# Weight conversion on VectorE and ScalarE alone, in 768-column jobs, in a gated linear attention with a feed-forward layer

## The chip, the cores and the metric

The kernel runs on one core of a Trainium2 chip. The metric is the device time of one execution in microseconds, as a median over executions; lower is better. A difference under about 0.5% (3 us here) can't be told from no change.

## The reference

The first stage is a gated linear attention over 4 batches, 8 heads, 768 time steps and head size 48. The second is a feed-forward layer over the 3072 tokens with 384 features each and an inner width of 2048. The two weights come in double precision, 8 bytes a number; everything else is float32.

```
for t in range(S):
    state = alpha[:, :, t, :, None] * state + einsum('bhd,bhe->bhde', k[:, :, t], v[:, :, t])
    y[:, :, t] = einsum('bhd,bhde->bhe', q[:, :, t], state)
x = y.transpose(0, 2, 1, 3).reshape(B * S, H * D)
h = x @ w_in
g = maximum(0.01 * h, h)
out = g @ w_out
```

## The kernel before

**Attention.** Time is cut into 6 chunks of 128 steps; a unit is one chunk of one batch, 24 in all, and three units make a block of 384 tokens. For a unit the generator `attention` yields eight slices of work: `scans` (running products of alpha on VectorE, L255 and L260), `scores` (TensorE, L292), `mask_scores` (one half masked by GpSimd at L299, one by VectorE at L302), `k_tokens` (L310), `scaled_q` and `scaled_k`, `outputs` (L326 and L332 on TensorE, then the float32r parts `xh` on ScalarE and `xl` on VectorE, L339), and `next_state` (the products of keys and values on TensorE, L353, then the state update by VectorE, L362, and GpSimd, L363). The first six units turn their inputs by TensorE (L227), the others by VectorE (L231). When the third unit of a block has its `xl`, `gather` sends six DMAs (L372) that complete the block's input, and the block is ready for the feed-forward.

**Feed-forward.** Every float32 number is split into a high and a low float32r part, and a product is three matmuls. An item (i, f) is slice f (128 of the 2048 inner columns, 16 slices) of block i (8 blocks): `ffn_in` does nine matmuls into `ph` (L413), ScalarE and VectorE make `t`, `gh`, `gl` (L416 to L421), and `ffn_out` does nine matmuls (L429), two items later (`LAG`).

**Weights.** Each of the 16 slices needs its part of `w_in` and of `w_out`. They are loaded as pairs of 32-bit words and turned into a high and a low part by integer work: 32 jobs of 384 columns, odd and even for the two weights, in three stages with a load ahead of them. Per job ScalarE does three operations (L177, L179, L200), VectorE three (L197, L198, L199), GpSimd two (L201, L202), and the last addition (L209) falls to GpSimd for odd jobs and to VectorE for even ones. Three buffers (`NRAW`) of 384 columns hold loaded words.

**Order of the work.** The program lists items in this order, with jobs and slices of attention between them, and a scheduler then sets each engine's order:

```
items = [(0, f, 2, SL / (CATCH - 1)) for f in range(CATCH)]
for n in range(LEAD):
    items += [(0, CATCH + n, 1, 0), (1, n, 1, 0)]
items += [(1, LEAD + n, 0, SL / (CATCH - 1) if n else 0) for n in range(CATCH)]
items += [(i, f, 0, SL / NF) for i in range(2, NB) for f in range(NF)]
```

The third entry is the number of calls of `convert`, the fourth the slices of attention beside the item. With `CATCH` 9 the first block runs alone for nine slices, then blocks 0 and 1 take turns for seven, then block 1 runs its last nine. Attention stops after unit 5 and goes on when block 0 is finished; the first five slices of it are held behind `gl` of item (0, 14) (`held`, `tc.issue_after`).

Of the kernel before, what the change touches and what calls it, by code (L numbers as in the profile page):

```python
# [22 lines left out]
def gated_linear_attn_ffn(ctx, tc, q, k, v, alpha, w_in, w_out, out):  # L23
# [30 lines left out]
    NREST, NBITS, NPW = 3, 3, 2  # L54
    NRAW = 3
# [4 lines left out]
    CATCH = 9  # L60
# [26 lines left out]
    wih, wil, woh, wol, x_sb = pieces("large", F32R, (NG, DF), (NG, DF), (NF, DM), (NF, DM), (2, 2 * NG + 1, TB))  # L87
# [65 lines left out]
    def load_weights(j):  # L153
        f, second = divmod(j, 2)
        wd = I64 if f64 else F32
        raw = cvp.tile([P, NG, 2 * P], I32, name="raw", bufs=NRAW)
        if second:
            dst = raw.rearrange("p g f -> p (g f)").bitcast(wd) if f64 else raw[:, :, 0:P].bitcast(F32)
            src = w_out[f * P:(f + 1) * P, :]
            nc.sync.dma_start(dst, src if f64 else src.rearrange("p (g f) -> p g f", g=NG))  # L160
        else:
            dst = raw.bitcast(wd) if f64 else raw[:, :, 0:P].bitcast(F32)
            for r, n, src, step in runs:
                a = w_in[src:src + n, f * P:(f + 1) * P]
                nc.sync.dma_start(
                    dst[r:r + n], bass.AP(a.tensor, a.offset, [list(a.ap[0]), [step * DF, NG], list(a.ap[1])])
                )
        jobs[j] = [raw]

    def convert_1(j):  # L170
        if not f64:
            return
        raw, = jobs[j]
        words = raw.rearrange("p g (f w) -> p g f w", w=2)
        top, low = words[:, :, :, 1], words[:, :, :, 0]
# [4 lines left out]
        jobs[j] = top, rest  # L180

    def convert_2(j):
        f, second = divmod(j, 2)
        if second:
            hi, lo = (w[:, f, :].rearrange("p (g f) -> p g f", g=NG) for w in (woh, wol))
        else:
            hi, lo = (w[:, :, f * P:(f + 1) * P] for w in (wih, wil))
        if not f64:
            val = jobs.pop(j)[0][:, :, 0:P].bitcast(F32)
            nc.scalar.copy(hi, val)  # L190
            nc.gpsimd.tensor_tensor(lo, val, hi.bitcast(F32), ALU.subtract)
            return
        top, rest = jobs[j]
        bits = cvp.tile([P, NG, P], I32, name="bits", bufs=NBITS)
        val = bits.bitcast(F32)
        pw = cvp.tile([P, NG, P], I32, name="pw", bufs=NPW)
# [3 lines left out]
        nc.scalar.copy(hi, val)  # L200
        nc.gpsimd.tensor_tensor(rest, pw.bitcast(F32), rest, ALU.mult)  # L201
        nc.gpsimd.tensor_tensor(val, val, hi.bitcast(F32), ALU.subtract)  # L202
        jobs[j] = lo, rest, val

    def convert_3(j):
        if f64:
            lo, rest, val = jobs.pop(j)
            eng = nc.gpsimd if j % 2 else nc.vector
            eng.tensor_tensor(lo, rest, val, ALU.add)  # L209

    NJ = 2 * NF

    def convert(h):
        for ahead, stage in ((5, convert_1), (4, convert_2), (2, convert_3), (8, load_weights)):
            if 0 <= h + ahead < NJ:
                stage(h + ahead)
# [98 lines left out]
    def outputs(u):  # L315
# [20 lines left out]
        del masked[u]  # L336
        xh, xl = (x_sb[0:BR, n, at:at + NP, j * C:(j + 1) * C] for n in (0, 1))
# [3 lines left out]
    def next_state(u):  # L341
        tb, b = units[u]
        pe, _, ktok = live.pop(u)[:3]
        V, W = vals_sb[u % NV], state[b]
        if tb == NC - 1:
            load_values(u + NV)
            return
        kv = bank()[:, 0:NP * D].rearrange("d (p e) -> d p e", p=NP)
        us = atp.tile([P, NP, D], F32, name="us") if tb else None
        for s, lo in ((0, 0), (1, HB)):  # L350
            for p in range(NP):
                h = 2 * p + s
                nc.tensor.matmul(  # L353
                    kv[lo:lo + D, p, :], ktok[:, p, lo:lo + D], V[:, h * D:(h + 1) * D], start=True, stop=True
                )
        load_values(u + NV)
# [49 lines left out]
    def ffn_in(i, f):  # L406
        xh, xl = xs[i]
        ph = ps_h.tile([P, 512], F32, name="ph")[:, 0:TB]
        fs = slice(f * P, (f + 1) * P)
        n = 0  # L410
        for g in range(NG):
            for wt, xt in ((wih, xh), (wih, xl), (wil, xh)):
                nc.tensor.matmul(ph, wt[:, g, fs], xt[:, g, :], start=n == 0, stop=n == 3 * NG - 1)  # L413
                n += 1
# [9 lines left out]
    def ffn_out(po, gs, f):  # L424
        gh, gl = gs
        for j in range(UPB):
            js = slice(j * C, (j + 1) * C)
            for n, (gt, wt) in enumerate(((gh, woh), (gh, wol), (gl, woh))):
                nc.tensor.matmul(  # L429
                    po[j], gt[:, js], wt[:, f, :], start=f == 0 and n == 0, stop=f == NF - 1 and n == 2  # L430
# [11 lines left out]
    for n in range(12):  # L442
        next(st)
        if n >= 4:
            convert(n - 12)
# [177 lines left out]
```

## Time and profile before

| | |
|---|---|
| median of 3 runs | 596.2 us (594.42 to 597.63) |
| the profiled execution | 594.61 us, of which the span is 592.9 us |
| busy share | PE 93%, weight loads 87%, DVE 70%, ACT 42%, POOL 23% |
| mean granted TensorE clock | 0.965 of 2.4 GHz |

The profiled execution is 1.6 us (0.3%) under the median. Busy shares are means over stages that differ: the first 220 us hold the weight conversion and nine units of attention, the rest is blocks 2 to 7 with the other units. A row of a timeline gives the start, the length, the engine, the line, the tiles, the number of merged instructions, and in brackets the idle time before it and what ended it. Rows of consecutive VectorE operations overlap by a little: the distance between two starts is what an operation holds the engine for.

### The profile page before, as it was taken

What the parts mean: (1) busy time and instruction counts of PE and PEld (TensorE: products, weight loads), DVE (VectorE), ACT (ScalarE), POOL (GpSimd) and SP (SyncE); (2) the same over time, 40 slices, a digit from 0 to 9 for tenths busy, and PEclk for the clock granted to TensorE, in tenths of its full rate; (3) what the DMA queues carried; (4) which work ended last, traced back from release to release, by engine and by line L of the source; (5) the groups of instructions that cost most, each with busy time, mean ns of one, the idle gap of its engine ahead of it and who ended that gap; (6) DMA issues with size and microseconds to landing.
All of it is one profiled execution on the core that took longest, in us unless ns stands there. A gap on an engine that the chain in (4) does not pass through costs nothing.

```text
span 592.9 us, 10070 instructions
## 1 busy us (share of the span) xinstructions
PE 550.6 (93%) x3706; PEld 516.1 (87%) x3706; DVE 414.2 (70%) x759; ACT 249.5 (42%) x541; POOL 138.7 (23%) x178
## 2 busy tenths in 40 slices
PE   5865989699999999999999999999999999999995
PEld 3754979598898879999999999999999989999995
DVE  6899999998999999356847775757757543333331
ACT  3666656554454335333534344333433243334332
POOL 3587679876001121011101001001101000000000
PEclk9877798889999999999999999999999999999998
DMA  9996763510434565014412251222311220011001
GB/s 164 209 192 165 168 170 89 158 50 1 112 109 103 127 137 135 22 39 83 116 37 62 60 131 45 62 51 59 102 26 39 46 67 0 2 21 40 2 1 44
DMA packets 90087, 48.11 MB, mean 81 GB/s; under 512 B 49584, under 2 KB 87984, under 8 KB 90032
## 3 DMA queue, kind: packets, MB, share of 16 engines
q1 hardware_dynamic: 90032, 47.41, 35.2%
q8 instruction: 31, 0.51, 0.3%
q14 instruction: 24, 0.20, 0.1%
HBM read 40.30 MB, written 4.72 MB: 76 GB/s over the span
## 4 chain that ended last, share of the span: by engine, by line
PE 64%; DVE 18%; DMA 7%; SPq 3%; issue 3%; POOL 1%; ACT 1%; DVEq 0%; ACTq 0%; POOLq 0%
PE ph L413 27%; PE a L429 27%; PE b L292 3%; PE b L332 2%; PE b L326 2%; DVE gl L421 2%; DVE bits L197 2%; DMA raw<-in_moe_w_in_dram 2%; DVE large L209 2%; DVE bits L198 2%; DMA large<-large 1%; DMA raw<-in_moe_w_out_dram 1%; DVE pc L255 1%; DMA small<-in_v_dram 1%; PE b L353 1%
## 5 line engine op out<-in xcount | busy, mean ns | idle before, releaser
L413 PE MATMUL ph<-large 128*128 128x384 f32 x1152 | 232.9, 346 | 9.6 <-DVE t L417 6.7
L413 PEld LDWEIGHTS ph<-large 128*128 128x128 f32 x1152 | 206.3, 193 | 15.8 <-DVE t L417 8.7
L429 PE MATMUL a<-large,gh 128*128 128x384 f32 x672 | 174.4, 344 | 0.0
L417 DVE TENSOR_TENSOR t<-ph,t 128x384 f32<-128x384 f32 x128 | 70.4, 552 | 100.3 <-ACT t L416 99.6
L429 PEld LDWEIGHTS a<-large,gh 128*128 128x128 f32 x672 | 119.3, 188 | 4.2 <-ACT gh L419 0.7
L416 ACT ACTIVATE t<-ph 128x384 f32<-128x384 f32 x128 | 62.4, 490 | 139.1 <-PE ph L413 131.2
L429 PE MATMUL a<-large,gl 128*128 128x384 f32 x336 | 110.7, 339 | 0.0
L421 DVE TENSOR_TENSOR gl<-t,gh 128x384 fp32r<-128x384 f32 x128 | 80.8, 632 | 39.6 <-ACT gh L419 37.5
L419 ACT CAST gh<-t 128x384 fp32r<-128x384 f32 x128 | 65.3, 513 | 80.2 <-DVE t L417 80.1
L363 POOL TENSOR_TENSOR small<-us,pe 48x192 f32<-48x192 f32 x32 | 18.3, 572 | 192.5 <-DVE us L362 191.8
L429 PEld LDWEIGHTS a<-large,gl 128*128 128x128 f32 x336 | 62.8, 188 | 0.2
L201 POOL TENSOR_TENSOR rest<-pw,rest 128x384 f32<-128x384 f32 x32 | 36.8, 1148 | 30.8 <-DVE pw L199 29.3
L299 POOL TENSOR_SCALAR_AFFINE_SELECT sm<-sm 128x512 f32<-128x512 f32 x24 | 17.5, 731 | 90.1 <-ACT sm L298 90.1
L202 POOL TENSOR_TENSOR bits<-bits,large 128x384 f32<-128x384 f32 x32 | 38.3, 1197 | 0.0
L266 ACT ACTIVATE e<-pc 128x512 f32<-128x512 f32 x24 | 15.2, 632 | 38.2 <-DVE rc L260 30.0
L292 PEld LDWEIGHTS b<-qs,ks 48*128 48x128 f32 x288 | 22.5, 187 | 8.7 <-issue 6.8
L292 PE MATMUL b<-qs,ks 48*128 48x128 f32 x288 | 28.4, 289 | 1.7 <-DVE us L362 0.8
L255 DVE TENSOR_TENSOR_SCAN pc<-e,small 128x128 f32<-128x128 f32 x72 | 25.5, 414 | 0.4
L429 PE MATMUL b<-large,gh 128*128 128x384 f32 x96 | 23.3, 345 | 2.1 <-ACT gh L419 2.1
L200 ACT CAST large<-bits 128x384 fp32r<-128x384 f32 x32 | 16.3, 511 | 20.5 <-DVE bits L198 20.2
L198 DVE SCALAR_TENSOR_TENSOR bits<-raw,bits 128x384 int32<-128x384 int32 x32 | 24.8, 789 | 0.2
L227 PE MATMUL a<-small 128*128 128x128 f32 x72 | 15.6, 367 | 8.9 <-POOL small L142 3.3
(80 smaller groups left out, 613.2 us busy)
## 6 DMA issues: line engine op xcount, KB each, us to landing
raw<-in_moe_w_out_dram SPq DMA_DIRECT2D x16, 384.0 KB, 3.8
small<-in_v_dram SPq DMA_DIRECT2D x24, 192.0 KB, 3.0
raw<-in_moe_w_in_dram SPq DMA_DIRECT2D x32, 144.0 KB, 3.9
out_dram<-t SPq DMA_DIRECT2D x24, 192.0 KB, 2.2
small<-in_alpha_dram SPq DMA_DIRECT2D x38, 96.0 KB, 2.3
small<-in_k_dram SPq DMA_DIRECT2D x36, 96.0 KB, 2.2
small<-in_q_dram SPq DMA_DIRECT2D x36, 96.0 KB, 2.2
small<-in_alpha_dram SPq DMA_DIRECT2D x36, 80.0 KB, 2.4
```

What stands on the lines that cost most here:

```text
L198: nc.vector.scalar_tensor_tensor(bits, top, -0x80000000, bits, ALU.bitwise_and, ALU.bitwise_or)
L201: nc.gpsimd.tensor_tensor(rest, pw.bitcast(F32), rest, ALU.mult)
L202: nc.gpsimd.tensor_tensor(val, val, hi.bitcast(F32), ALU.subtract)
L255: nc.vector.tensor_tensor_scan(pc[:, p, :], aT[:, p, :], ones.broadcast_to([P, C]), 1.0, ALU.mult, ALU.mult)
L292: nc.tensor.matmul(ss[s][:, p, :], ks[lo:lo + D, p, :], qs[lo:lo + D, p, :], start=True, stop=True)
L363: nc.gpsimd.tensor_tensor(W[r, :, r], us[r], pe[r].broadcast_to([D, NP, D]), ALU.mult)
L413: nc.tensor.matmul(ph, wt[:, g, fs], xt[:, g, :], start=n == 0, stop=n == 3 * NG - 1)
L416: nc.scalar.mul(t, ph, 0.01)
L417: nc.vector.tensor_tensor(t, ph, t, ALU.max)
L419: nc.scalar.copy(gh, t)
L421: made[i, f] = nc.vector.tensor_tensor(gl, t, gh.bitcast(F32), ALU.subtract)
L429: nc.tensor.matmul(po[j], gt[:, js], wt[:, f, :], start=f == 0 and n == 0, stop=f == NF - 1 and n == 2)
```

## The change

All of the conversion's GpSimd work goes to VectorE, and one job now holds slice f of both weights side by side, 768 columns wide: for one slice of both weights ScalarE does two operations of 768 columns instead of six of 384, and VectorE six of 768 columns instead of seven of 384. The low words are scaled and multiplied in one VectorE operation. The load buffers stay three, each twice as wide; the weights lie in `wh` and `wl` with both parts of a slice beside each other. `CATCH` goes from 9 to 6, with one `convert` call for each of the first 26 items, of which the first 15 still find a stage to run. In `outputs` the eight products of keys and values (`kv`) are issued right behind the value products, ahead of `xh` and `xl`, and in pairs of halves; before they were issued in the slice after.

```diff
-    CATCH = 9
+    CATCH = 6
...
-    def load_weights(j):
-        f, second = divmod(j, 2)
+    def load_weights(f):
...
-        raw = cvp.tile([P, NG, 2 * P], I32, name="raw", bufs=NRAW)
+        raw = cvp.tile([P, 2 * NG, 2 * P], I32, name="raw", bufs=NRAW)
...
-        rest = cvp.tile([P, NG, P], F32, name="rest", bufs=NREST)
-        nc.scalar.activation(rest, low.bitcast(U32), AF.Copy, scale=2.0 ** -52)
         nc.scalar.mul(top.bitcast(F32), top.bitcast(F32), 2.0 ** -112)
...
+        bits = cvp.tile([P, 2 * DM], I32, name="bits", bufs=NBITS)
+        pw = cvp.tile([P, 2 * DM], I32, name="pw", bufs=NPW)
         nc.vector.tensor_scalar(bits, top, 3, 0x7FFFFFF8, ALU.logical_shift_left, ALU.bitwise_and)
         nc.vector.scalar_tensor_tensor(bits, top, -0x80000000, bits, ALU.bitwise_and, ALU.bitwise_or)
+        nc.scalar.copy(hi, val)
         nc.vector.tensor_scalar(pw, bits, -0x800000, None, ALU.bitwise_and)
-        nc.scalar.copy(hi, val)
-        nc.gpsimd.tensor_tensor(rest, pw.bitcast(F32), rest, ALU.mult)
-        nc.gpsimd.tensor_tensor(val, val, hi.bitcast(F32), ALU.subtract)
+        nc.vector.scalar_tensor_tensor(rest, low.bitcast(U32), 2.0 ** -52, rest, ALU.mult, ALU.mult)
...
-            eng = nc.gpsimd if j % 2 else nc.vector
-            eng.tensor_tensor(lo, rest, val, ALU.add)
+            nc.vector.tensor_tensor(val, val, hi.bitcast(F32), ALU.subtract)
+            nc.vector.tensor_tensor(lo, rest, val, ALU.add)
...
     def convert(h):
-        for ahead, stage in ((5, convert_1), (4, convert_2), (2, convert_3), (8, load_weights)):
+        for ahead, stage in ((2, convert_1), (2, convert_2), (1, convert_3), (4, load_weights)):
...
+                    nc.tensor.matmul(
+                        kv[lo:lo + D, p, :], ktok[:, p, lo:lo + D], V[:, h * D:(h + 1) * D], start=True, stop=True
+                    )
+        load_values(u + NV)
+        live[u] = pe, kv
         xh, xl = (x_sb[0:BR, n, at:at + NP, j * C:(j + 1) * C] for n in (0, 1))
         nc.scalar.copy(xh, y[0:BR])
...
-        if n >= 4:
-            convert(n - 12)
+        if n in (4, 6, 8, 10):
+            convert(n // 2 - 6)
...
-    items = [(0, f, 2, SL / (CATCH - 1)) for f in range(CATCH)]
+    items = [(0, f, 1, SL / (CATCH - 1)) for f in range(CATCH)]
```

Three places show what the scheduler makes of it. In the kernel before, VectorE's last conversions lie among the feed-forward's operations (`t` and `gl` of an item), and three pairs follow the last one (L209) until the attention of unit 6 begins (L231):

```order
L199 TENSOR_SCALAR pw_1580<-bits_1579 128x384
L417 TENSOR_TENSOR t_1525<-ph_1515,t_1525 128x384
L421 TENSOR_TENSOR gl_1530<-t_1525,gh_1528 128x384
L209 TENSOR_TENSOR large_74<-rest_1503,bits_1544 128x3x128
L417 TENSOR_TENSOR t_1563<-ph_1553,t_1563 128x384
L421 TENSOR_TENSOR gl_1568<-t_1563,gh_1566 128x384
```

In the changed kernel VectorE's order behind the `xl` of unit 5 (L347, the operation that lets block 1's input be gathered) holds only conversions for a while: the slices of jobs 10 to 13 stand there and no item of the feed-forward:

```order
L347 TENSOR_TENSOR large_74<-a_797,large_74 112x4x128
L208 TENSOR_TENSOR large_74<-pw_1006,bits_1005 128x768
L201 SCALAR_TENSOR_TENSOR pw_1048<-raw_972,pw_1048 128x768
L207 TENSOR_TENSOR bits_1047<-bits_1047,large_74 128x768
L197 TENSOR_SCALAR bits_1089<-raw_1014 128x768
L208 TENSOR_TENSOR large_74<-pw_1048,bits_1047 128x768
L198 SCALAR_TENSOR_TENSOR bits_1089<-raw_1014,bits_1089 128x768
L197 TENSOR_SCALAR bits_1131<-raw_1056 128x768
L200 TENSOR_SCALAR pw_1090<-bits_1089 128x768
L198 SCALAR_TENSOR_TENSOR bits_1131<-raw_1056,bits_1131 128x768
L201 SCALAR_TENSOR_TENSOR pw_1090<-raw_1014,pw_1090 128x768
```

Seven items of the feed-forward have their `gl` ahead of this place; in the kernel before eight had it ahead of the same `xl`. Further on in the changed kernel, behind the last conversion, nine pairs of `t` and `gl` stand alone before the attention of unit 6 begins (L228); the last two are these:

```order
L415 TENSOR_TENSOR t_1438<-ph_1428,t_1438 128x384
L419 TENSOR_TENSOR gl_1443<-t_1438,gh_1441 128x384
L415 TENSOR_TENSOR t_1464<-ph_1454,t_1464 128x384
L419 TENSOR_TENSOR gl_1469<-t_1464,gh_1467 128x384
L228 STREAM_TRANSPOSE e_1610<-small_73 128x4x4x32
L228 STREAM_TRANSPOSE qs_1630<-small_73 128x4x4x32
```

So the conversions moved forward and the `gl` of item (0, 14), which is the last before L228 in either kernel, became the 23rd item's instead of the 20th's. On TensorE the third place is unit 7 in the kernel before, where the products of keys and values (L353) stand behind nine matmuls of the feed-forward:

```order
L326 MATMUL b<-qs,small 112x128 x4
L332 MATMUL b<-sm,small 48x128 x8
L413 MATMUL ph<-large 128x384 x9
L353 MATMUL b<-small,ktok 48x48 x8
L429 MATMUL a<-large,gh 128x384 x2
```

In the changed kernel they follow the value products of the same unit:

```order
L323 MATMUL b<-qs,small 112x128 x4
L329 MATMUL b<-sm,small 48x128 x8
L340 MATMUL b<-small,ktok 48x48 x8
L411 MATMUL ph<-large 128x384 x9
```

From block 2 to the end TensorE goes back and forth between feed-forward and attention 104 times in the changed kernel and 120 times in the one before.

## Rows read from the trace of the kernel before

**Rows 1.** The page, part 1: busy time of each engine, share of the span, instructions.

```profile
PE 550.6 (93%) x3706; PEld 516.1 (87%) x3706; DVE 414.2 (70%) x759; ACT 249.5 (42%) x541; POOL 138.7 (23%) x178
```

**Rows 2.** Busy time of each engine by stretch, granted clock, DMA share, GB/s.

```profile
61.00:105.00 44.00, 40.32 (x272) 38.26 (x270) 42.62 (x70) 26.40 (x58) 34.01 (x32) 0.90 0.56 137
105.00:151.00 46.00, 39.82 (x196) 37.72 (x197) 40.91 (x60) 22.93 (x49) 33.00 (x29) 0.89 0.25 67
151.00:209.40 58.40, 54.91 (x407) 51.15 (x405) 57.31 (x113) 25.39 (x60) 6.38 (x15) 1.00 0.49 120
...
278.00:343.50 65.50, 65.50 (x469) 61.63 (x468) 44.30 (x84) 25.89 (x57) 6.07 (x12) 1.00 0.32 75
```

**Rows 3.** Groups of VectorE instructions from 15 to 151 us: count | busy, mean ns.

```profile
L198 DVE SCALAR_TENSOR_TENSOR bits<-raw,bits 128x384 int32<-128x384 int32 x32 | 24.8, 789 | 0.2
L421 DVE TENSOR_TENSOR gl<-t,gh 128x384 fp32r<-128x384 f32 x20 | 19.6, 978 | 4.5 <-ACT gh L419 4.5
L197 DVE TENSOR_SCALAR bits<-raw 128x384 int32<-128x384 int32 x32 | 18.4, 588 | 0.8 <-ACT raw L179 0.8
L209 DVE TENSOR_TENSOR large<-rest,bits 128x384 fp32r<-128x384 f32 x16 | 17.8, 1116 | 0.1
L199 DVE TENSOR_SCALAR pw<-bits 128x384 int32<-128x384 int32 x32 | 16.7, 534 | 0.1
```

**Rows 4.** Groups of VectorE instructions from 240 us to the end.

```profile
L421 DVE TENSOR_TENSOR gl<-t,gh 128x384 fp32r<-128x384 f32 x90 | 50.6, 564 | 34.1 <-ACT gh L419 31.9 <-PE a L429 2.0
```

**Rows 5.** Timeline of VectorE: operations that start back to back.

```profile
29.21 0.55 DVE L198 SCALAR_TENSOR_TENSOR bits<-raw,bits 128x384 int32<-128x384 int32 x1
29.68 0.35 DVE L197 TENSOR_SCALAR bits<-raw 128x384 int32<-128x384 int32 x1
29.95 0.72 DVE L360 TENSOR_TENSOR small<-a,pe 48x192 f32<-48x192 f32 x2
...
52.44 0.68 DVE L275 TENSOR_TENSOR qs<-a,pc 128x512 f32<-128x512 f32 x1
53.04 0.68 DVE L283 TENSOR_TENSOR ks<-a,rc 128x512 f32<-128x512 f32 x1
```

**Rows 6.** Timeline of VectorE: an even job's last addition, and one held up.

```profile
78.70 0.54 DVE L209 TENSOR_TENSOR large<-rest,bits 128x384 fp32r<-128x384 f32 x1
...
102.16 1.36 DVE L209 TENSOR_TENSOR large<-rest,bits 128x384 fp32r<-128x384 f32 x1
```

**Rows 7.** Timeline of VectorE: marks of units 5 and 8, item (0, 14), block 2.

```profile
104.20 0.69 DVE L339 TENSOR_TENSOR large<-a,large 112x512 fp32r<-112x512 f32 x1
...
150.25 0.56 DVE L421 TENSOR_TENSOR gl<-t,gh 128x384 fp32r<-128x384 f32 x1 [0.58 <-ACT gh L419]
...
208.73 0.69 DVE L339 TENSOR_TENSOR large<-b,large 112x512 fp32r<-112x512 f32 x1
...
219.94 0.55 DVE L417 TENSOR_TENSOR t<-ph,t 128x384 f32<-128x384 f32 x1
```

**Rows 8.** Timeline of TensorE: after an idle stretch, and a change to attention and back.

```profile
118.23 6.13 PE L413 MATMUL ph<-large 128*128 128x384 f32 x18 [2.79 <-DVE t L417]
...
386.46 1.16 PE L292 MATMUL b<-qs,ks 48*128 48x128 f32 x16
387.55 0.62 PE L429 MATMUL a<-large,gh 128*128 128x384 f32 x2
...
388.18 0.51 PE L429 MATMUL a<-large,gh 128*128 128x384 f32 x2
```

**Rows 9.** DMA issues of SyncE for a gather; landing times of all gathers, 40 to 130 us.

```profile
45.40 3.07 SPq L372 DMA_DIRECT2D large<-large  x4
...
DMA to landing us min/median/max: 2.1/2.2/3.3
```

**Rows 10.** The chain that ended last, near the end: start, length, what.

```profile
559.49 1.59 PE a L429 x9
561.08 1.56 PE ph L413 x9
```

More of the change, by code (lines that the diff above doesn't have):

```diff
@@ L53, in gated_linear_attn_ffn @@
     NV = 2
-    NREST, NBITS, NPW = 3, 3, 2
-    NRAW = 3
+    NBITS, NPW, NRAW = 2, 2, 3
     T4 = 4
@@ L170, in convert_1 @@
-    def convert_1(j):
+        raw = cvp.tile([P, 2 * NG, 2 * P], I32, name="raw", bufs=NRAW)
+        if f64:
+            dst = raw.bitcast(wd)
+        else:
+            dst = raw[:, :, 0:P].bitcast(wd)
+        for r, n, src, step in runs:
+            a = w_in[src:src + n, f * P:(f + 1) * P]
+            nc.sync.dma_start(
+                dst[r:r + n, 0:NG], bass.AP(a.tensor, a.offset, [list(a.ap[0]), [step * DF, NG], list(a.ap[1])])
+            )
+        nc.sync.dma_start(dst[:, NG:], w_out[f * P:(f + 1) * P, :].rearrange("p (g f) -> p g f", g=NG))
@@ L171, in convert_1 @@
+        jobs[f] = [raw]
+    def convert_1(f):
         if not f64:
             return
-        raw, = jobs[j]
-        words = raw.rearrange("p g (f w) -> p g f w", w=2)
-        top, low = words[:, :, :, 1], words[:, :, :, 0]
-        rest = cvp.tile([P, NG, P], F32, name="rest", bufs=NREST)
-        nc.scalar.activation(rest, low.bitcast(U32), AF.Copy, scale=2.0 ** -52)
-        nc.scalar.mul(top.bitcast(F32), top.bitcast(F32), 2.0 ** -112)
[L180 to L187, printed above, removed]
-        if not f64:
-            val = jobs.pop(j)[0][:, :, 0:P].bitcast(F32)
-            nc.scalar.copy(hi, val)
-            nc.gpsimd.tensor_tensor(lo, val, hi.bitcast(F32), ALU.subtract)
+        raw, = jobs[f]
+        words = raw.rearrange("p g (f w) -> p (g f) w", w=2)
+        top, low = words[:, :, 1], words[:, :, 0]
+        nc.scalar.mul(top.bitcast(F32), top.bitcast(F32), 2.0 ** -112)
+        jobs[f] = top, low
@@ L342, in next_state @@
         tb, b = units[u]
[L343 to L346, printed above, removed]
+        pe, kv = live.pop(u)
+        if kv is None:
             return
-        kv = bank()[:, 0:NP * D].rearrange("d (p e) -> d p e", p=NP)
+        W = state[b]
         us = atp.tile([P, NP, D], F32, name="us") if tb else None
[L350 to L356, printed above, removed]
         for lo in (0, HB):
@@ L408, in ffn_in @@
         ph = ps_h.tile([P, 512], F32, name="ph")[:, 0:TB]
-        fs = slice(f * P, (f + 1) * P)
         n = 0
         for g in range(NG):
-            for wt, xt in ((wih, xh), (wih, xl), (wil, xh)):
-                nc.tensor.matmul(ph, wt[:, g, fs], xt[:, g, :], start=n == 0, stop=n == 3 * NG - 1)
+            for wt, xt in ((wh, xh), (wh, xl), (wl, xh)):
+                nc.tensor.matmul(ph, w_in_of(wt, f, g), xt[:, g, :], start=n == 0, stop=n == 3 * NG - 1)
                 n += 1
@@ L427, in ffn_out @@
             js = slice(j * C, (j + 1) * C)
-            for n, (gt, wt) in enumerate(((gh, woh), (gh, wol), (gl, woh))):
+            for n, (gt, wt) in enumerate(((gh, wh), (gh, wl), (gl, wh))):
                 nc.tensor.matmul(
-                    po[j], gt[:, js], wt[:, f, :], start=f == 0 and n == 0, stop=f == NF - 1 and n == 2
+                    po[j], gt[:, js], w_out_of(wt, f), start=f == 0 and n == 0, stop=f == NF - 1 and n == 2
                 )
@@ L584, in stepwise @@
                     nc.vector.tensor_tensor(gl, g, gh.bitcast(F32), ALU.subtract)
-                    for n, (gt, wt) in enumerate(((gh, woh), (gh, wol), (gl, woh))):
-                        nc.tensor.matmul(po, gt, wt[:, f, :], start=f == 0 and n == 0, stop=f == NF - 1 and n == 2)
+                    for n, (gt, wt) in enumerate(((gh, wh), (gh, wl), (gl, wh))):
+                        nc.tensor.matmul(po, gt, w_out_of(wt, f), start=f == 0 and n == 0, stop=f == NF - 1 and n == 2)
                 o = gp.tile([P, DM], F32, name="o")
```

52 lines of the change are left out of this document (27 added, 25 removed).

## The prediction

> **What bounds the kernel now.** I read the busy times by stretch first, then the groups of VectorE, then the two timelines around the places where the attention of one block must be complete before the next block can begin. From block 2 on the kernel is a TensorE kernel: a block with three units beside it takes 65.5 us, TensorE is busy in all of them at the full clock, and VectorE has 21 us to spare [rows 2]. An item costs 1.56 us for its first nine matmuls and 1.59 for the other nine [rows 10]. Nothing that VectorE gains there moves the end. The first 220 us are different. From 61 to 209.4 us VectorE is busy 140.8 of 148.4 us, TensorE 135.1, the latter in part at a granted clock of 0.9 [rows 2]. So the front is VectorE's, with TensorE close behind, and what counts is when three marks are reached [rows 7]: the `xl` of unit 5 (104.2 us), which lets block 1 begin; the `gl` of item (0, 14), over at 150.8 us, behind which the attention of units 6 to 8 is held; and the `xl` of unit 8 (208.7 us), after which block 2's first `t` comes at 219.9. I price the change at each mark.
>
> **What the conversion costs VectorE.** GpSimd's 138.7 us [rows 1] are mostly conversion, and they are not free for VectorE: the same addition of 384 columns takes 0.54 us at one place and 1.36 at another [rows 6], and `gl` takes 978 ns on average while the conversion runs and 564 after it [rows 3, 4]. In the stretch of the conversion VectorE spends 24.8 + 18.4 + 16.7 + 17.8 = 77.7 us on it [rows 3]. Undisturbed, an operation with two inputs holds the engine for 0.47 us at 384 columns (29.21 to 29.68) and 0.60 at 512 (52.44 to 53.04), so 1.04 ns a column and 0.87 us at 768; the one with a constant 0.27 at 384 (29.68 to 29.95), so 0.47 at 768 at the same 0.07 of fixed time [rows 5]. A new job is two of the second kind and four of the first: 0.94 + 3.48 = 4.4 us, 16 jobs 70.7 us. The old ones overlap their neighbours by some 0.08 us each (0.55 against 0.47), 112 of them 9 us, so they held the engine for about 69. The conversion itself therefore costs VectorE the same as before; taking the work over is paid for by the blocking that goes away. The gain is on `gl`: 20 times 0.41, 8.3 us. The operation that scales the low words has no row; its bounds are 0.47 us (the cheap kind) and 1.36 (the held-up kind at 384), and I take 0.87 since it reads two tensors as L198 does: 16 times the difference is -6 to +8 us.
>
> The Trainium skill, in "SBUF — State Buffer", section "Who interferes with whom", says why: GpSimd and VectorE's second port are one pair, and an operation with two SBUF inputs that meets a GpSimd operation reading SBUF is blocked for the whole of it. By that rule the selects and state updates that stay on GpSimd could each still block one of the long new operations, at 0.7 us each some 8 us over the eleven units in the front. The row speaks for less: from 240 us on the same selects and updates run beside 90 `gl` that take 564 ns on average, next to the shortest seen [rows 4, 5]. The sum goes by the row, at nothing.
>
> **First mark.** Up to the `xl` of unit 5 the old order has 22 jobs' three stages and 11 additions on VectorE, the new one 12 jobs' first three operations, 11 of the next two each and 10 of the last. Old: 22 times (0.789 + 0.588 + 0.534 - 3 times 0.08) plus 11 times 1.03, 48 us [rows 3]. New: 12 times (0.94 + 0.87) plus 32 times 0.87, 49.6 us. Items: eight pairs of `t` and `gl` at 0.47 + 0.90, 11 us, against seven at 0.94, 6.6. That is 2.8 us less, 101.4. New waits come in: the second job needs all of both weights of slice 1 at about 20 us, when only half of that was needed before, and the transposes of unit 4 stand on TensorE behind the first 18 matmuls of the feed-forward. I put 1.5 and 1 us on them and come to 104 us; bounds 101 (no wait) and 107 (each twice as long, and one of TensorE's clock restarts in it).
>
> **Second mark.** This is where `CATCH` costs. The 23rd item's `gl` is now the one that releases attention, not the 20th's, and 16 items' first matmuls stand between block 1's gather and it. From the `xl`: two DMA issues at 0.77 us and 2.2 to land [rows 9], 3.7 us. Then TensorE has 16 times 1.56 and 13 times 1.59 to do, 45.6 us [rows 10]. It stood idle for some 5 us before, since VectorE then does conversions only (the second fence on the order); before, after 2.8 us idle, 18 matmuls took 6.13 us where two times 1.56 is 3.1 [rows 8], so 3 us more. Then `t` to `gl`, four operations of about 0.55 us, 2.2. Sum 54.5 us, and the mark lies at 158.5 us instead of 150.8: +7.7. VectorE's own work in that stretch (26 us of conversions and seven pairs, and then nine pairs that wait for TensorE at 3.15 us an item) ends within a microsecond or two of the same time, so neither is far off the path.
>
> **Third mark.** Between the two marks VectorE was busy 57.3 of 58.4 us [rows 2]. Its work there is the same but for three pairs of `t` and `gl` that are now done earlier (2.8 us) and a transpose and a few small operations that stand later (1.3 us): -4.1. From the `xl` of unit 8 to block 2's first `t` the new order has about 1.2 us less on VectorE: -1.2. Behind that everything is TensorE's. It changes 16 times less between attention and feed-forward; a change and back costs 0.1 us at 386.46 (the items before end at 386.36) and 0.11 on return (0.62 against 0.51) [rows 8], so 8 pairs save 1.7 us. And some 15 small products of unit 9 are already done, 0.7 us. This is what the move of the `kv` products is worth; the pairing of halves I price at nothing, since each keeps its weight load.
>
> **Sum.** +7.7 - 4.1 - 1.2 - 1.7 - 0.7 = 0.0 us on a profile of 594.6 us. The median of before lies 1.6 us higher, at 596.2, and so does the forecast: 596.2 us. VectorE loses its obstruction, and the time comes back as TensorE's: conversions that run ahead of need, then fourteen items in a row that nothing can shorten.
>
> **Rivals.** *Faster, 0.30:* the front is not stopped by TensorE. If the first mark comes at 101 and TensorE isn't cold when block 1 begins (its 3 us), the second mark falls at 152.5 and the end at 590. The 8.3 us of `gl` and GpSimd's freedom speak for it (masks and state updates no longer queue behind 1.2 us operations); TensorE's 40.3 busy of 44 us from 61 to 105 speaks against it [rows 2]. *Slower, 0.27:* VectorE is stopped by what TensorE owes it. It takes its list in order, and with GpSimd gone every conversion now stands in that one list: a `t` whose `ph` is late holds back the slice that a later `ph` needs. The place is from the first items to the end of the conversions, where VectorE had 1.4 us idle of 44 [rows 2]. If it waits 3 us more ahead of the first mark and 3 more behind it, the end is at 602; from 1.5 us in each it is measurable. *No difference, 0.43:* the sum. Loads bring the same bytes; by the sum the conversions end near 131 us where the last one now ends near 145, so they are wanted at a rate about a tenth higher than now, and a slice that comes late counts with the slower case.
>
> **Range.** The low end takes the faster rival and a cheaper scale operation, 588.5; the high end the slower one and some of the remaining blocking, 604. Faster by over 0.5% 0.30, same 0.43, slower 0.27; 3 us is about the least that can be told here.
>
> **What would show it.** The new operations at 0.95 us (0.87 held) and `gl` at 0.56 from the start; GpSimd's busy time near 35 us; the `xl` of unit 5 at 101 to 107; TensorE at a low clock just after, and then without a gap while VectorE idles for nine items; the `gl` before the transposes at 156 to 161; unit 8's `xl` at 210 to 214; blocks of about 65 us. It is wrong if the long operations are held up by what is left on GpSimd, if VectorE shows waits for `ph` or raw data of over 6 us from 20 to 130 us, or if attention starts well ahead of 155.

## The result and the profile after

The changed kernel takes 600.88 us (median of 6 runs, 598.73 to 602.2) against 596.58 us before (6 runs): ratio 1.0076, 95% interval 1.0049 to 1.0103. It is slower by 4.3 us, where no change was forecast; the time lies inside the range. The profiled execution of after took 602.2 us (span 600.4), that of before 594.6: 7.6 us between the two, and these are what the marks below add up to. The first lies 1.3 us above its median and the second 2.0 below, so 3.3 of the 7.6 us are spread between executions and not the change. All times are medians; in one experiment a single execution of 1685 us is left out.

The page of after, busy time of each engine (answers to [rows 1]):

```profile
PE 552.5 (92%) x3706; PEld 521.5 (87%) x3706; DVE 406.2 (68%) x743; ACT 231.2 (39%) x477; POOL 51.6 (9%) x98
```

GpSimd has lost 87 us and VectorE is not busier. Busy time by stretch for after (answers to [rows 2]: PE, PEld, DVE, ACT, POOL, granted clock, DMA share, GB/s):

```profile
0.00:61.00 61.00, 36.17 (x229) 29.50 (x230) 50.79 (x98) 24.09 (x43) 10.84 (x26) 0.72 1.00 176
61.00:105.00 44.00, 39.56 (x298) 36.93 (x297) 43.02 (x74) 21.51 (x39) 5.35 (x8) 0.92 0.67 151
105.00:165.00 60.00, 52.86 (x277) 52.58 (x278) 39.39 (x63) 21.38 (x39) 0.71 (x1) 0.89 0.19 48
165.00:220.00 55.00, 51.23 (x375) 46.20 (x373) 52.44 (x105) 22.83 (x54) 6.52 (x14) 0.98 0.52 124
...
137.00:165.00 28.00, 28.00 (x161) 28.00 (x160) 10.32 (x19) 9.05 (x18) 0.00 (x0) 1.00 0.00 1
```

The third row and the last are the new thing: for 60 us VectorE is busy 39.4, and in the last 28 of them TensorE runs without a gap while VectorE is busy for 10.3. Before, VectorE had 40.9 busy of 46 us there [rows 2].

VectorE's groups of after from 15 to 165 us (answers to [rows 3]):

```profile
L198 DVE SCALAR_TENSOR_TENSOR bits<-raw,bits 128x768 int32<-128x768 int32 x16 | 15.5, 967 | 0.0
L208 DVE TENSOR_TENSOR large<-pw,bits 128x768 fp32r<-128x768 f32 x16 | 15.4, 962 | 0.1
L201 DVE SCALAR_TENSOR_TENSOR pw<-raw,pw 128x768 f32<-128x768 uint32 x16 | 15.2, 950 | 0.0
L207 DVE TENSOR_TENSOR bits<-bits,large 128x768 f32<-128x768 f32 x16 | 15.2, 949 | 0.3 <-ACT large L199 0.3
L415 DVE TENSOR_TENSOR t<-ph,t 128x384 f32<-128x384 f32 x23 | 12.7, 552 | 15.4 <-ACT t L414 15.4
L419 DVE TENSOR_TENSOR gl<-t,gh 128x384 fp32r<-128x384 f32 x23 | 12.7, 554 | 5.8 <-ACT gh L417 5.7
L197 DVE TENSOR_SCALAR bits<-raw 128x768 int32<-128x768 int32 x16 | 9.2, 577 | 2.8 <-ACT raw L181 2.7 <-DMA large<-large 0.2
L200 DVE TENSOR_SCALAR pw<-bits 128x768 int32<-128x768 int32 x16 | 8.8, 550 | 0.1
```

The six groups of the conversion (L197 to L208) add up to 79.3 us, against 77.7 before; less 0.08 us of overlap for each of the 96 operations it is 71.6 us held, and 70.7 were forecast. `gl` fell from 978 to 554 ns. So every operation has the price that it was given. What moved is when things are reached. The marks of after in VectorE's timeline, `xl` of units 1, 2, 3 and 5, the last `gl` ahead of the held attention, `xl` of unit 8, and block 2's first `t` (answers to [rows 7]):

```profile
37.72 0.68 DVE L347 TENSOR_TENSOR large<-a,large 112x512 fp32r<-112x512 f32 x1
55.55 0.69 DVE L347 TENSOR_TENSOR large<-a,large 112x512 fp32r<-112x512 f32 x1 [0.39 <-ACT large L346]
74.34 0.68 DVE L347 TENSOR_TENSOR large<-a,large 112x512 fp32r<-112x512 f32 x1
...
105.42 0.69 DVE L347 TENSOR_TENSOR large<-a,large 112x512 fp32r<-112x512 f32 x1
...
164.16 0.56 DVE L419 TENSOR_TENSOR gl<-t,gh 128x384 fp32r<-128x384 f32 x1 [0.58 <-ACT gh L417]
...
219.21 0.69 DVE L347 TENSOR_TENSOR large<-b,large 112x512 fp32r<-112x512 f32 x1
...
229.74 1.08 DVE L415 TENSOR_TENSOR t<-ph,t 128x384 f32<-128x384 f32 x2 [0.66 <-ACT t L414]
```

Before, units 1 to 3 had their `xl` at 31.1, 44.7 and 58.6 us: after is late by 6.6, 10.9 and 15.8 us, and only the shorter first block brings unit 5 back to 105.4 (104.2 before). The second mark, 164.7 against 150.8, is 13.9 us late; the third 10.5 us; and from there to the end after takes 381.2 us against 384.2. So 10.5 lost and 3.0 won, the 7.6 us up to rounding.

TensorE of after behind the first mark (answers to [rows 8]):

```profile
102.41 1.07 PE L329 MATMUL a<-sm,small 128*48 128x128 f32 x14
110.39 5.86 PE L411 MATMUL ph<-large 128*128 128x384 f32 x18 [6.90 <-DMA large<-large]
118.00 2.21 PE L411 MATMUL ph<-large 128*128 128x384 f32 x9 [1.75 <-DVE t L415]
120.01 2.12 PE L427 MATMUL a<-large,gh 128*128 128x384 f32 x6
121.93 2.07 PE L411 MATMUL ph<-large 128*128 128x384 f32 x9
```

It waits 6.9 us for the gather of block 1, does 18 matmuls in 5.86 us where the full clock needs 3.1, waits 1.75 for a `t`, and is still slow in the next three groups. The granted clock (the column behind POOL's) is 0.54 in the first of these stretches, so 1.2 GHz for most of it, 0.72 in the second, and 1.00 from 124 us on:

```profile
110.30:116.30 6.00, 5.86 (x18) 5.58 (x18) 5.59 (x8) 2.52 (x4) 0.00 (x0) 0.54 0.82 207
118.00:124.00 6.00, 6.00 (x25) 6.00 (x26) 6.00 (x10) 3.35 (x6) 0.00 (x0) 0.72 0.02 4
```

The `t` is late because ScalarE comes to it only at 116.9 us: ahead of it in ScalarE's order stands the scaling of a slice of raw weights, which waits 2.25 us for their load to land.

```profile
116.10 0.88 ACT L181 ACTIVATE raw<-raw 128x768 f32<-128x768 f32 x1 [2.25 <-DMA raw<-in_moe_w_in_dram]
```

SyncE's queue ahead of the gather (answers to [rows 9]):

```profile
104.58 1.85 SPq L168 DMA_DIRECT2D raw<-in_moe_w_in_dram  x4
106.53 3.78 SPq L371 DMA_DIRECT2D large<-large  x6
```

The gather's first issue (L371) follows four issues for a slice of weights and starts 0.4 us behind the end of `xl` (105.42 + 0.69).

### The profile page after: what moved, and what is told of

It reads as the page before. It is cut to its first block, busy times and chain, and to the rows that moved or that the text cites. A ratio compares the mean times of both kernels' runs of the same rounds, so it can differ in the third digit from the quotient of the medians.

```text
span 600.4 us, 9923 instructions
## 1 busy us (share of the span) xinstructions
PE 552.5 (92%) x3706; PEld 521.5 (87%) x3706; DVE 406.2 (68%) x743; ACT 231.2 (39%) x477; POOL 51.6 (9%) x98
## 4 chain that ended last, share of the span: by engine, by line
PE 74%; DVE 11%; DMA 7%; SPq 3%; ACT 2%; issue 2%; ACTq 0%; DVEq 0%
PE ph L411 32%; PE a L427 28%; PE b L289 3%; PE b L427 3%; PE b L329 3%; PE b L323 2%; DMA raw<-in_moe_w_in_dram 2%; DMA small<-in_alpha_dram 1%; DMA small<-in_q_dram 1%; DMA raw<-in_moe_w_out_dram 1%; DVE pc L252 1%; DVE e L228 1%; DVE qs L228 1%; SPq L168 1%; PE b L340 1%
## 5 line engine op out<-in xcount | busy, mean ns | idle before, releaser
L427 PE MATMUL a<-large,gh 128*128 128x384 f32 x672 | 172.6, 344 | 0.0
L427 PEld LDWEIGHTS a<-large,gh 128*128 128x128 f32 x672 | 121.0, 189 | 2.6 <-ACT gh L417 0.2
L419 DVE TENSOR_TENSOR gl<-t,gh 128x384 fp32r<-128x384 f32 x128 | 70.8, 554 | 43.9 <-ACT gh L417 43.7
L362 POOL TENSOR_TENSOR small<-us,pe 48x192 f32<-48x192 f32 x32 | 19.2, 600 | 198.3 <-DVE us L361 196.9
L296 POOL TENSOR_SCALAR_AFFINE_SELECT sm<-sm 128x512 f32<-128x512 f32 x24 | 17.8, 741 | 178.1 <-ACT sm L295 178.0
L289 PE MATMUL b<-qs,ks 48*128 48x128 f32 x288 | 31.7, 291 | 0.4 <-DVE us L361 0.4
L289 PEld LDWEIGHTS b<-qs,ks 48*128 48x128 f32 x288 | 25.0, 188 | 7.9 <-issue 6.5
L224 PEld LDWEIGHTS a<-small 128*128 128x128 f32 x72 | 11.8, 195 | 20.7 <-DVE ks L280 4.0
L181 ACT ACTIVATE raw<-raw 128x768 f32<-128x768 f32 x16 | 14.6, 914 | 37.3 <-DMA raw<-in_moe_w_in_dram 24.3
L257 DVE TENSOR_TENSOR_SCAN rc<-e,rc,small 128x511 f32<-128x511 f32 x18 | 23.3, 1293 | 0.5
L228 DVE STREAM_TRANSPOSE ks<-small 128x512 f32<-128x512 f32 x18 | 19.9, 1112 | 4.6 <-PE b L307 4.6
L329 PE MATMUL b<-sm,small 128*48 128x128 f32 x288 | 22.2, 286 | 0.6 <-DVE sm L299 0.6
```

Of the source, the lines that this page charges most:

```text
L224: nc.tensor.transpose(ps[:, p, :], by_token(src)[:, 2 * p:2 * p + 2, :].rearrange("t h d -> t (h d)"), ident)
L228: nc.vector.transpose(t.rearrange("r p (j t) -> r p t j", t=T4), src.rearrange("r p (t d) -> r p t d", t=T4)[:, :, :, 0:32],)
L257: nc.vector.tensor_tensor_scan(flat[2][:, NP * C - 2::-1], flat[0][:, NP * C - 1:0:-1], flat[1][:, NP * C - 2::-1], rc[:, NP - 1, C - 1:C] ...
L289: nc.tensor.matmul(ss[s][:, p, :], ks[lo:lo + D, p, :], qs[lo:lo + D, p, :], start=True, stop=True)
L329: nc.tensor.matmul(y[lo:lo + m, r, :], V[:, c:c + m], masked[u][s][:, p, :], start=not tb and p == 0, stop=p == NP - 1, skip_group_check=True,
L419: made[i, f] = nc.vector.tensor_tensor(gl, t, gh.bitcast(F32), ALU.subtract)
```

## The experiments

All ratios are to the kernel before, run beside each kernel; its medians were 595.6 to 596.4 us. Marks and waits are read from one profiled execution of each kernel; it lies within 2 us of the median, but 3.5 us under it for the kernel with smaller buffers and `CATCH` 9. "Halves" counts weights of 384 columns, so that a job of 768 is two; a "split" is an `xl`. At first the suspicion was on `CATCH` alone (Theory A); the later theories came out of the runs before them.

**`CATCH` alone**, in the kernel before.

```diff
-    CATCH = 9
+    CATCH = 6
```

> The kernel before with CATCH 6 and nothing else. Theory A (the loss comes from CATCH: the attention of unit 6 is released by the 23rd item instead of the 20th, behind items that TensorE works off at 3.15 us each after a cold start): 600 to 603 us, with the gl before the first transposes at 157 to 163 us instead of 150.8 and unit 8's xl some 5 us later. Theory B (the loss comes from giving VectorE all of the conversion): 596 to 597, as before. Theory C (the products of keys and values right behind the value products cost it): as before.

Measured: 599.3 us, ratio 1.0061 (1.0041 to 1.008). Its marks:

```profile
96.12 0.69 DVE L339 TENSOR_TENSOR large<-a,large 112x512 fp32r<-112x512 f32 x1
160.67 1.10 DVE L231 STREAM_TRANSPOSE e<-small 128x512 f32<-128x512 f32 x1
213.81 0.69 DVE L339 TENSOR_TENSOR large<-b,large 112x512 fp32r<-112x512 f32 x1
```

Three items fewer bring the first mark 8 us forward, and the attention held behind item (0, 14) starts 10 us later all the same. With the old conversion `CATCH` 6 costs 3.6 us, a little less than Theory A had (600 to 603 us).

**The changed kernel with `CATCH` 9.**

```diff
-    CATCH = 6
+    CATCH = 9
```

> The changed kernel with CATCH 9. Theory A: faster than both, 591 to 594 us: the first mark comes later than in the changed kernel (two more items ahead of it), near 108 us, the gl before the transposes at 150 to 153, unit 8's xl near 209. Theory B: 599 to 602, as the changed kernel. Theory C: 599 to 602.

Measured: 596.04 us, ratio 1.0003 (0.9987 to 1.0019); `xl` of unit 5 at 110.7, transposes at 151.4, `xl` of unit 8 at 211.3. It gains 4.8 us over the changed kernel but does not fall below before: the conversion and the move of the products together are worth nothing, which Theory A (591 to 594 us) had not said.

**An earlier release of the held attention**, in the changed kernel.

```diff
-                with tc.issue_after(made[0, NF - 2].ins) if held else nullcontext():
+                with tc.issue_after(made[0, NF - 6].ins) if held else nullcontext():
```

> The changed kernel with the first five slices of unit 6's attention held behind gl of item (0, 10) instead of (0, 14), 8 items earlier in the order. Theory A: VectorE's idle time between 137 and 165 us is filled with transposes and scans, unit 8's xl comes 6 to 10 us earlier than 219, and the time is 591 to 595. Theory B: VectorE has no room, less than 2 us gained, 599 to 601. Theory C: no difference from the changed kernel beyond 2 us.

Measured: 596.45 us, ratio 1.0018 (0.9996 to 1.0039); transposes at 139.0 instead of 164.6, `xl` of unit 8 at 214.5 instead of 219.2. VectorE's idle time ahead of the second mark is real time lost, but a release 25 us earlier gives back only 4.7 us at the third mark, less than Theory A had.

**The products back in `next_state`**, the rest as changed: the eight `kv` matmuls and `load_values` move out of `outputs` again.

> The changed kernel with the products of keys and values back in the slice after the outputs, in the old order of halves. Theory A: 601 to 603, 1 to 2 us slower than the changed kernel, since about 8 more changes between attention and feed-forward at 0.2 us come back. Theory B: the same as A. Theory C: faster than the changed kernel by 3 to 4 us, 596 to 598.

Measured: 604.45 us, ratio 1.0151 (1.0127 to 1.0176). So in the changed kernel the move gains 3.6 us, and Theory C, which puts the loss on it, falls.

**The new conversion alone:** the changed kernel with `CATCH` 9 and the products back.

> The new conversion alone: the changed kernel with CATCH set back to 9 and the state products back in next_state. Theory A (the three parts add up, each near 3.6 us): the conversion costs by itself, since with CATCH 9 and the products moved the time was that of before and the move was worth 3.6 us; so 599 to 601 us, 0.5% to 0.9% above before, lost ahead of the first transposes of the held attention, and already in the first 60 us. Rival D (the move of the products is worth 3.6 us only where VectorE is crowded, so the parts do not add up): 596 to 598 us, at most 0.3% above. What the prediction said (a conversion on VectorE costs nothing and the gelu's subtraction gains 8 us): 588 to 593 us.

Measured: 599.99 us, ratio 1.0065 (1.0043 to 1.0086). What the forecast held to be a gain of 8 us is a loss of 3.9. This is the run that decides against Rival D (596 to 598 us).

**The move of the products alone**, in the kernel before.

> The kernel before with the state products issued right behind the value products, and nothing else changed. Theory A: 592 to 593.5 us, 0.5% to 0.7% below before, won in the attention of blocks 2 and later, behind 220 us, where each change of TensorE to attention work and back ends one wait earlier. Rival D: 594 to 595.5 us, 0.2% to 0.4% below, as the prediction priced it (1.7 to 2.4 us). The first two marks (the last split of unit 5 near 104, the last gelu subtraction ahead of the transposes near 151 us) stay within 1 us under both.

Measured: 593.72 us, ratio 0.9953 (0.9933 to 0.9972). This lies between Theory A (592 to 593.5 us) and Rival D (594 to 595.5). The three parts alone multiply to 1.0061 x 1.0065 x 0.9953 = 1.0079, and the whole change is 1.0076: within their intervals they add up.

**Products moved and the earlier release, on the kernel before.**

> The kernel before with the state products moved and the held attention behind item (0, 10) instead of item (0, 14). Theory A: the hold costs VectorE idle time that is paid back later, so letting go four items earlier is worth what it was worth in the changed kernel (4.4 us) less what before already has between its first and second marks (its wait is shorter by 12 us), so 588 to 592 us, transposes at 138 to 143 us instead of 151. Rival E (an early release gives the attention to VectorE while the gelu of the first pair of blocks needs it, so TensorE waits instead): 592 to 596 us, the first transposes earlier but unit 8's split no earlier than 207 us.

Measured: 594.21 us, ratio 0.9971 (0.9957 to 0.9984), no better than the move alone.

```profile
123.01 1.10 DVE L231 STREAM_TRANSPOSE e<-small 128x512 f32<-128x512 f32 x1
...
211.04 0.69 DVE L350 TENSOR_TENSOR large<-b,large 112x512 fp32r<-112x512 f32 x1
```

The transposes come 27.5 us earlier than in the move alone, unit 8's `xl` 2.5 us later. Between the first two marks of the kernel before VectorE is idle for only 5 of 46 us [rows 2], so there is little for early attention to fill, and it buys nothing. Rival E had this, and the waits of TensorE that it named are there: for `t` 8.8 us between the first and third marks, against 6.4 in the move alone.

**GpSimd's part of the conversion on VectorE, in the old halves**, with the products moved and `CATCH` 9.

```diff
-        nc.gpsimd.tensor_tensor(rest, pw.bitcast(F32), rest, ALU.mult)
-        nc.gpsimd.tensor_tensor(val, val, hi.bitcast(F32), ALU.subtract)
+        nc.vector.tensor_tensor(rest, pw.bitcast(F32), rest, ALU.mult)
+        nc.vector.tensor_tensor(val, val, hi.bitcast(F32), ALU.subtract)
...
-            eng = nc.gpsimd if j % 2 else nc.vector
+            eng = nc.vector
```

> The kernel before with the state products moved, and the three conversion operations of GpSimd put on VectorE in the old jobs of 384 columns (two-input operations of 384 columns, so 80 more of them, about 0.5 us each, 40 us, less what the gelu's subtraction gains). Theory A1 (what the new conversion costs is VectorE time in the first 60 us and between 60 and 105 us, whatever the size of the jobs): 597 to 602 us. Theory A2 (it costs by its size: operations of 768 columns keep short attention operations waiting, and weights of an item come later): 592 to 595 us, near the move of the products alone.

Measured: 582.67 us, ratio 0.9782 (0.9759 to 0.9805), the fastest of all and far under both theories. Against the move alone that is 0.9782 / 0.9953 = 0.983, 10 us won by taking the conversion off GpSimd. Its groups from 15 to 165 us, its marks of units 2, 3 and 5, and its stretches:

```profile
L209 DVE TENSOR_TENSOR large<-rest,bits 128x384 fp32r<-128x384 f32 x32 | 17.5, 566 | 0.1
L198 DVE SCALAR_TENSOR_TENSOR bits<-raw,bits 128x384 int32<-128x384 int32 x32 | 17.2, 551 | 0.0
L423 DVE TENSOR_TENSOR gl<-t,gh 128x384 fp32r<-128x384 f32 x25 | 13.8, 553 | 0.0
```
```profile
48.51 0.68 DVE L350 TENSOR_TENSOR large<-a,large 112x512 fp32r<-112x512 f32 x1
64.26 0.69 DVE L350 TENSOR_TENSOR large<-a,large 112x512 fp32r<-112x512 f32 x1
...
96.61 0.69 DVE L350 TENSOR_TENSOR large<-a,large 112x512 fp32r<-112x512 f32 x1
```
```profile
61.00:105.00 44.00, 41.45 (x294) 37.80 (x293) 43.77 (x103) 26.20 (x57) 3.91 (x7) 1.00 0.55 133
105.00:151.00 46.00, 40.81 (x225) 39.10 (x226) 44.71 (x104) 26.49 (x58) 0.19 (x1) 1.00 0.40 100
```

An operation of the conversion falls from 789 or 1116 ns [rows 3] to 551 or 566, `gl` from 978 to 553. VectorE stays busy through both stretches, and TensorE holds its full clock in them. So a gain like the forecast's 8.3 us is to be had, and the form of the new conversion throws it away. Two readings were left. Theory P: its place, since buffers for whole slices let conversion run ahead of the attention units in VectorE's order. Rival S: its size, since operations of 768 columns hold up the short ones of the attention. The next runs tell these apart.

**Halves with larger buffers.**

```diff
-    NREST, NBITS, NPW = 3, 3, 2
-    NRAW = 3
+    NREST, NBITS, NPW = 4, 4, 4
+    NRAW = 6
```

> The conversion on VectorE in halves of 384 columns (582.7 us with 3 raw, 3 rest, 3 bits and 2 pw buffers) with 6, 4, 4 and 4: the operations stay, but 24 half-weights are started ahead of unit 5's last split instead of 19, and 17 instead of 12 ahead of unit 3's, nearly as in the changed kernel. Theory P: unit 5's split at 105 to 109 instead of 96.6 us and 592 to 597 us. Rival S: 581 to 585 us.

Measured: 593.54 us, ratio 0.9953 (0.9937 to 0.9969): 10.9 us above the same operations with fewer buffers. Its marks of units 2, 3 and 5:

```profile
56.32 0.68 DVE L350 TENSOR_TENSOR large<-a,large 112x512 fp32r<-112x512 f32 x1
74.32 0.69 DVE L350 TENSOR_TENSOR large<-a,large 112x512 fp32r<-112x512 f32 x1
...
109.93 0.69 DVE L350 TENSOR_TENSOR large<-a,large 112x512 fp32r<-112x512 f32 x1
```

Units 2 and 3 come within 1 us of the changed kernel's. Nothing in an operation was altered, only how far conversion may run ahead: Theory P, and not Rival S (581 to 585 us). The changed kernel with `CATCH` 9, which starts 26 halves ahead of unit 5 where this one starts 24, takes 596.0 us: at nearly the same run-ahead the two sizes are 2.5 us apart.

**The changed kernel with smaller conversion buffers,** nothing else.

```diff
-    NBITS, NPW, NRAW = 2, 2, 3
+    NBITS, NPW, NRAW = 1, 1, 2
```

> The changed kernel itself (CATCH 6) with the smaller conversion buffers alone: 16 half-weights started ahead of unit 5's last split instead of 24. Theory P: 587 to 592 us, some 3.6 us above the same with CATCH 9 and 9 to 13 us below the changed kernel. Rival S: 599 to 602 us.

Measured: 586.97 us (584.3 to 592.7), ratio 0.9868 (0.9824 to 0.9913): 13.9 us below the changed kernel (12.4 by the ratios, since two of the six executions took 592 us). Conversions begun ahead of unit 3's `xl`, first in the changed kernel (to 74.3 us), then here (to 62.2 us; groups of VectorE):

```profile
L198 DVE SCALAR_TENSOR_TENSOR bits<-raw,bits 128x768 int32<-128x768 int32 x8 | 7.6, 945 | 0.0
```
```profile
L198 DVE SCALAR_TENSOR_TENSOR bits<-raw,bits 128x768 int32<-128x768 int32 x5 | 4.7, 936 | 0.0
```

Its marks of unit 5, the held attention and unit 8:

```profile
90.67 0.69 DVE L347 TENSOR_TENSOR large<-a,large 112x512 fp32r<-112x512 f32 x1
...
152.49 1.10 DVE L228 STREAM_TRANSPOSE e<-small 128x512 f32<-128x512 f32 x1
...
204.19 0.69 DVE L347 TENSOR_TENSOR large<-b,large 112x512 fp32r<-112x512 f32 x1
```

And what VectorE waited for between its first and second marks, the changed kernel (105 to 165 us) first, then this one (90 to 153 us):

```profile
DVE t L415 <- ACT t L414: 15.1, 10, 2.0
DVE gl L419 <- ACT gh L417: 5.2, 9, 0.6
```
```profile
DVE t L415 <- ACT t L414: 4.1, 3, 2.5
```

Three jobs fewer stand ahead of unit 3, so units 3 and 5 come 12 and 15 us earlier; these jobs are then done where VectorE used to wait for TensorE, 4 us of waits instead of 20.

**The same buffers with `CATCH` 9.**

> The changed kernel with CATCH 9, with one buffer instead of two for bits and pw and two instead of three for raw: the operations and their widths stay, but VectorE's program now starts 16 half-weights (8 jobs of 768) ahead of the last split of unit 5, where with CATCH 9 and the larger buffers it starts 26, and the conversion in halves (582.7 us) starts 19. Theory P (what the new conversion loses is its place: buffers for whole items let it run ahead of the attention units in VectorE's order, and VectorE idles later): unit 5's split by 98 instead of 110.7 us, transposes by 146, 584 to 589 us. Rival S (operations of 768 columns lose by their length, each holding up short attention operations): 594 to 597 us, as with the larger buffers.

Measured: 591.26 us (587.8 to 592.5), ratio 0.9917 (0.9894 to 0.9939). It has 4.8 us less than with the larger buffers, and unit 5's `xl` (91.6 us for P's 98) and the transposes (147.1 for 146) come much earlier than the larger buffers' 110.7 and 151.4, but the time is a little above P's range, and of unit 5's 19 us the median keeps 5.

**Only `bits` and `pw` with one buffer; only `raw` with two.** The two halves of the edit, each in the changed kernel.

> The changed kernel with one buffer each for bits and pw; raw keeps three. VectorE's program starts 16 half-weights ahead of unit 5's last split, as with two raw buffers besides (16), where the changed kernel starts 24; the loads can still run three items ahead. Theory P (VectorE's order): 585 to 590 us, as with all the smaller buffers. Theory Q (the raw loads crowd the attention's loads, on SP's queue and the DMA engines): 597 to 601 us, since the loads run ahead as before.

> The changed kernel with two raw buffers instead of three; bits and pw keep two. VectorE's program starts 14 half-weights ahead of unit 3's last split (16 in the changed kernel, 10 with the small buffers) and 20 ahead of unit 5's (24 and 16). Theory P: between the two, 593 to 597 us. Theory Q: 586 to 590 us, since the loads are held back as with all the smaller buffers.

Measured: 591.49 us, ratio 0.9899 (0.9868 to 0.993), and 601.79 us, ratio 1.0084 (1.0067 to 1.0102). The run-ahead goes by way of `bits` and `pw`; holding back the loads alone gains nothing, so Theory Q falls. P missed the first by 1.5 us (585 to 590 expected) and the second more clearly (593 to 597 expected): unit 5 came 5.7 us earlier, at 99.7, but the transposes only at 165.2. VectorE's waits there, 99 to 165 us:

```profile
DVE t L415 <- ACT t L414: 8.6, 6, 1.5
DVE bits L197 <- ACT raw L181: 6.0, 4, 2.9
DVE gl L419 <- ACT gh L417: 3.5, 6, 0.6
DVE bits L197 <- DMA large<-large: 2.6, 1, 2.6
```

VectorE now waits 6.0 us for raw weights to be scaled, and ScalarE, which scales them, waits 13.4 us in these 66 us for their loads to land, against 3.2 us from 100 to 165 us in the changed kernel: with two buffers the loads come too late.

**Halves with two of each buffer.**

> The conversion on VectorE in halves with 2 of each buffer: 15 half-weights started ahead of unit 5's last split instead of 19. Theory P: unit 5's split 3 to 5 us earlier (92 to 94 us); 580 to 583 us, unless TensorE then waits for weights in the stretch behind it, then 584 to 588 us. Rival S: 581 to 585 us, unit 5's split unmoved.

Measured: 586.31 us, ratio 0.9838 (0.9812 to 0.9864); unit 5 at 86.3 us, 10 us earlier, unit 8 at 201.2 instead of 199.2. Too little run-ahead costs as well: the held attention starts where it did (143.8 and 142.9). Between these marks TensorE waits 3.8 us for converted weights (`large` from ScalarE), which it does not in the halves with more buffers; P had named this case, at 584 to 588 us.

**Halves with `CATCH` 6.**

> The conversion on VectorE in halves, state products moved (582.7 us), with CATCH 6 in place of 9. Theory P with CATCH at its price in the kernel before (3.6 us): 585 to 588 us. Rival (CATCH costs only where VectorE is the later one at the second mark; with the conversion's order mended the price is gone, as the two runs with the smaller buffers suggest, 587.0 with 6 and 591.3 with 9): 578 to 583 us.

Measured: 589.4 us (four executions), ratio 0.9872 (0.9848 to 0.9896): `CATCH` costs 5.4 us by the ratios and 6.7 by the medians here, more than P had, and the rival falls.

## Why the prediction was wrong

**The conversion's place, not its price.** The step that failed is the second mark's term of the sum, "the mark lies at 158.5 us instead of 150.8: +7.7"; it measured +13.9. Under it lies another: "The conversion itself therefore costs VectorE the same as before; taking the work over is paid for by the blocking that goes away." In microseconds of VectorE that is right (79.3 against 77.7, `gl` back at 0.55). In the kernel it is not: the new conversion alone costs 3.9 us, nearly the whole miss, since `CATCH` (3.6 lost) and the products (2.2 won, 2.8 by the ratio) almost cancel. The sum counted what stands ahead of the first mark, but priced it as work and not for its place. With two `bits`, two `pw` and three `raw` buffers, each for a whole slice, VectorE does 38.5 us of conversion ahead of unit 3's `xl`, 25.7 in the kernel before (durations of its timeline added up). In halves on VectorE alone, with as many weights begun there as before (12 halves), it is 33.0: of the 12.8 us, 7.3 are work taken over and 5.5 run-ahead. The attention of units 1 to 3 moves back by 7 to 16 us, and VectorE is idle for 20 us later. The forecast's own last words on it, "conversions that run ahead of need", were priced only as 1.6 us more work ahead of unit 5. The runs give the run-ahead two prices: 10.9 us with nothing but buffers changed in halves, 12 to 14 us in the changed kernel. With less of it, the conversion on VectorE is worth 10 us; the forecast had 8.3, but that these are the same microseconds is not shown.

**First mark, 104 forecast, 105.4 measured:** right, and in its terms. From 15 us on, counted from start to start, conversion held VectorE for 50.8 us (49.6 forecast) and 47.2 before (48), items for 6.6 (6.6) and 11.4 (11), and VectorE was idle 1.8 us more (2.5). What the forecast took as given, 12 jobs ahead of this mark, was where the time lay: with `CATCH` 6 and the old conversion the mark comes at 96.1, with the smaller buffers at 90.7.

**Second mark, 158.5 forecast, 164.7 measured.** From the first mark 59.3 us instead of 54.5, and the first mark 1.4 late. The rows name 4.4 of these 4.8 us. TensorE starts the matmuls of block 1 at 5.0 us behind the start of `xl` and not at 3.7: 0.7 of this is the length of `xl` itself, which the sum left out, 0.4 the weight loads ahead of the gather in SyncE's queue. The 1.75 us for the late `t`, behind raw weights that ScalarE waits for, were priced at nothing. The low clock takes about 1.6 from the 24 matmuls behind that wait, less 0.3 on the first 18. The mechanism was as forecast, fourteen items that nothing shortens with VectorE idle; the size was not.

**Third mark and the rest.** 54.5 us from the second mark, 53.8 forecast; 3.0 us won behind it, 3.6 forecast: right. The products' move is worth 2.2 us alone (2.8 by the ratio, 2.4 forecast) and 3.6 in the changed kernel.

**Rivals.** The slower one had the right side and about the right time (602 forecast), mostly by another way: from 15 to 105 us VectorE waited 2.3 us more than before (5.7 against 3.4), which the sum's own 2.5 cover; the late `t` behind raw weights is its kind of wait, at 1.75 us. The faster one, 590 if the first mark came early and TensorE stayed warm, is near what the smaller buffers show: unit 5 at 90.7, TensorE waiting 2.5 us for the gather instead of 6.9, 587.0 us. Of the three things that were to show the forecast wrong none appeared: long operations held up, over 6 us of waits for `ph` or raw data from 20 to 130 us (4.3 came), attention well ahead of 155 us. What missed its mark is unit 8's `xl`, at 219.2 us instead of 210 to 214.

**What GpSimd still does** (51.6 us; about 35 forecast) blocked little: the long operations take 949 to 967 ns on average, the shortest seen 927. Three of the 96 conversion operations are drawn out beside its work, to 1258 and 1192 ns during state updates (L362) and 987 instead of 550 during a select (L296), about 1 us in all. The Trainium skill, "SBUF — State Buffer", section "Who interferes with whom", describes the blocking that the old conversion showed, and the trace agrees for what was removed (978 to 554 ns). Of the 8 us that the rule allowed for the selects and state updates left on GpSimd, about 1 appears.

**Open.** `CATCH` 6 cost 3.6 to 6.7 us in three pairs of runs and seems to gain 3 to 4 with the smaller buffers (587.0 against 591.3 us, executions spread over 8 and 5 us); this was not settled. Nor is whether the third `raw` buffer costs anything once `bits` and `pw` have one: 591.5 with it and 587.0 without, with intervals that overlap. Nor is how much of the 8.6 us between few buffers with 768 columns and halves (591.3 and 582.7, both `CATCH` 9) is the length of the operations and how much their single buffers.

## What to carry to other kernels

When work moves to an engine that takes its list in order, price where it stands in that list, not only how long it takes: count what is started ahead of each mark on which another engine depends. Buffers set that place: one fewer of each of three was worth 12 to 14 us here, as much as the change of engine itself or more. But too few cost as well: halves with two `raw`, `rest` and `bits` were 3.6 us slower than with three. An engine that turns idle in the stretch behind its busiest one can be a sign that it did too early what could have waited; it is no proof, since `CATCH` 6 alone left VectorE idle for 13 of 65 us between the first two marks.

## What the runs showed of the hardware

An operation of two 384-column inputs in SBUF took 1116 ns on average beside GpSimd's conversion and 566 with it gone, operations with a constant 588 and 355 ns [rows 3]. So 92 us of conversion operations in 32 halves on VectorE alone (all six groups, 15 to 165 us) finished a kernel 11 us sooner than 77 us of them with GpSimd's help (the move of the products alone). And a low clock cost more than the first groups behind the idle time. After 6.9 us of waiting TensorE did 18 matmuls of the changed kernel at a granted clock of 0.54, 2.7 us lost; behind a wait of 1.75 us more it did the next 24, 118 to 124 us, at 0.72, about 1.6 us lost.
